# Keys of the next batch transposed earlier, in the PSUM bank of the AV products, with eight buffers instead of six

## Chip, cores and metric

The kernel runs on one core of one Trainium2 chip. The metric is the time of one execution on the device in microseconds; of several runs the median counts. The engines are named as the profile names them: PE (TensorE), DVE (VectorE), ACT (ScalarE), POOL (GpSimd), SP (SyncE, which here only issues DMA transfers). PEld is TensorE's loading of weights.

## What is computed

Attention with head mixing, then a routed mixture of experts, then a dense layer pair, on 4 batches of 448 tokens, 12 heads of 64. Only the first part bears on this change:

```python
scale = 1.0 / np.sqrt(q.shape[-1])
scores = scale * np.matmul(q, k.transpose(0, 1, 3, 2))
scores = np.einsum('bhij,hg->bgij', scores, w_pre)
scores = scores - np.max(scores, axis=-1, keepdims=True)
attn = np.exp(scores)
attn = attn / (np.sum(attn, axis=-1, keepdims=True) + 1e-09)
attn = np.einsum('bhij,hg->bgij', attn, w_post)
return np.matmul(attn, v).astype(np.float32)
```

The result, one row of 768 per token, goes to eight experts (`relu(x @ w1) @ w2`, the best expert of each token alone, weighted by its gate), and what comes out to `(h - tanh(h)) @ w_out` with `h = x @ w_in`.

## The kernel before

Each batch's 448 query rows are cut into tiles of 120, 120, 120 and 88 rows, 16 tiles T in all (T = 4b to 4b+3 are batch b's). A tile goes through these steps, named as in the code and, for their tiles, in the trace:

- `tr_q` (L297) turns the tile's queries for three pairs of heads at once into a PSUM bank (ptq); ACT copies them out as the high half qh (L304), DVE subtracts to get the low half ql (L305). `tr_k` (L281) does the same for the keys of one pair of heads and one whole batch: ptk, then kh on ACT (L287) and kl on DVE (L288). A pair is turned once per batch, six pairs in each.
- `emit_S` (L324) makes the scores of one pair of heads from three products (kh with qh, kl with qh, kh with ql). `emit_S2` makes two pairs: the first into the double bank "a", the second, one head each, into banks "d" and "e". ACT and DVE write them, scaled, to `ssb` in SBUF.
- A DMA on SP's queue (the relay, L354, seven rounds ahead) regroups ten query rows with all twelve heads on 120 partitions (`sr`). That is a block; the 16 tiles have 180, twelve or nine to a tile, 45 to a batch.
- For each block: P mixes the heads (L367, bank "b"); DVE takes the maximum (L369), ACT the exponential (L372); DVE makes the second mixing matrix with the row sums in it, w (L379 to L382); two rounds later T mixes and transposes (L404, bank "c") and ACT copies to A (L409).
- `emit_AV2` (L422) multiplies a whole tile's A by v for two pairs, into bank "d"; ACT copies that to xT (L424). `emit_X` (L456) turns xT and makes the router's products, half a tile at a time, in bank "e".
- `emit_R` routes the tokens of a batch, with small steps on DVE and PE. `conv_do` (L115 to L121) prepares weights of the dense part on DVE and POOL, about every second round.

Banks: PSUM has tags "a" (two banks), "b" and "c" (two each), "d" and "e" (one each). A tile in "d" or "e" can be written only when everybody has read the one before it there.

The order of instructions is written out. The loop over rounds s emits P of block s, then at most one score or AV step (`emit_S`, `emit_S2`, `emit_AV2`), then T of block s-2, then what else the round has: `tr_q`, `tr_k`, `emit_X`. Which round a step falls into is worked out ahead by `posS2`, `posAV` and the functions `at` and `at_e`; `at_e` moves a step to the next round that no other user of bank "e" has taken. The reading of such a late step's bank is put off to the next round: ACT's copy comes first in that round, DVE's part behind the reduce of the round's P and behind w. In these lines of the loop `flush()` gives out ACT's copies and `flush2()` DVE's subtractions:

```python
flush()
relay_to(s + NSR - 1)
ex = emit_P(s) if s < NBK else lambda: None
if 0 <= s - 1 < NBK:
    emit_W(s - 1)
flush2()
```

After the rounds come the experts, with their own pools in the memory that the attention stage gives back, and the dense layers.

Of the kernel before, what the change touches and what calls it, by code (L numbers as in the profile page):

```python
# [9 lines left out]
F32R = mybir.dt.float32r  # L10
# [20 lines left out]
def body(ctx: ExitStack, tc, q, k, v, w_pre, w_post, emb, tau, w1, w2, win, wout, out):  # L31
    nc = tc.nc
    pe, act, dve, pool, sp = nc.tensor, nc.scalar, nc.vector, nc.gpsimd, nc.sync
    B, H, S, D = q.shape
    NT = B * S
    DM = H * D
    E, _, FF = w1.shape
    F2 = wout.shape[0]
    CP, NJ = 112, 4
    NP = H // 2  # L40
# [13 lines left out]
    def ps(tag, nm):  # L54
        if len(PB) > 1:
            tag = {"a": "h", "b": "h"}.get(tag, "o")
        return psum[-1].tile([128, 512], F32, tag=tag, name=nm, bufs=PB[-1][tag])
# [67 lines left out]
    if True:  # L125
# [3 lines left out]
        ap = bctx.enter_context(tc.tile_pool(name="attnB", bufs=1, side="left"))  # L129
# [147 lines left out]
        def tr_k(b, p, tag="e"):  # L277
            src = nat.pop(("k", b, p))
            pt = ps(tag, f"ptk{b}_{p}")
            for c in range(NJ):  # L280
                pe.transpose(pt[:, c * CP:(c + 1) * CP], src[:, c].rearrange("p h d -> p (h d)"), ident[:CP, :CP])  # L281
            hi = ap.tile([128, S], F32R, tag="kh", name=f"kh{b}_{p}", bufs=6)
            lo = ap.tile([128, S], F32R, tag="kl", name=f"kl{b}_{p}", bufs=6)
            kT[b, p] = (hi, lo)

            def evac():
                act.copy(hi, pt[:, :S])  # L287
                return lambda: dve.tensor_sub(lo, pt[:, :S], hi.bitcast(F32))  # L288
            return evac
# [45 lines left out]
        for T in range(4 * B):  # L335
            n = IT[T % 4][1]
# [74 lines left out]
        xT = {}  # L411

        def emit_AV(T, p, cpy=act.copy, m=1):
            b, it = divmod(T, 4)
            n = IT[it][1]
            if p == 0:
                xT[T] = cp.tile([128, KD, 120], F32, tag="xT", name=f"xT{T}", bufs=2)
            pt = ps("d", f"AV{T}_{p}")
            for x in range(m):
                for c in range(NJ):  # L420
                    for hh in range(2):
                        pe.matmul(pt[64 * hh:64 * hh + 64, x * 120:x * 120 + n], vt[b, p + x][:, hh, c, :],  # L422
                                  A[T][:, c, 2 * (p + x) + hh, :n], start=c == 0, stop=c == NJ - 1)
            return lambda: cpy(xT[T][:, p:p + m, :n], pt[:, :m * 120].rearrange("d (x i) -> d x i", x=m)[:, :, :n])  # L424

        def emit_S2(T, p):

# [8 lines left out]
        def emit_AV2(T, p):  # L436
            return emit_AV(T, p, act.copy, 2)
# [174 lines left out]
    with mctx:  # L612
# [240 lines left out]
        def at(pos, fn, *a):  # L853
            side.setdefault(int(pos), []).append((fn, a))
# [3 lines left out]
        def at_e(pos, fn, *a):  # L858
            pos = int(pos)
            while pos in eused:  # L860
                pos += 1
            eused.add(pos)
            at(pos, fn, *a)
            return pos

        def posS(T, p):
            f, nb = (first[T - 1], ntile[T - 1]) if T else (-12, 12)
            return f - (5 if T > 1 else 3) + (p + 0.5) * nb / 6

        def posS2(T, p):  # L870
            return posS(T, p - p % 2 + 0.5)

        def posAV(T, p):
            f, nb = first[T + 1], ntile[T + 1]
            return f + LAG + 1 + p * nb / 6

        def at_s(pos, *a):
            pos = int(pos)
            eused.add(pos)
            at(pos, *a)  # L880

        for T in range(1, 4 * B):
            if T == 1:
                at_s(posS(T, 3), emit_S, T, 3)
                at_s(posS(T, 4), emit_S2, T, 4)
            else:
                for p in range(0, NP, 2):
                    at_s(posS2(T, p), emit_S2, T, p)
        for T in range(2, 4 * B):
            at(posS2(T, 0) - 6, load_q, T)  # L890
            at_e(posS2(T, 0) - 2, tr_q, T, 0)
            at_e(posS2(T, 2) - 2, tr_q, T, 1)
        for b in range(1, B):
            for p in range(NP):
                e = posS2(4 * b - 1, p) + 1
                at(e - 5, load_k, b, p)
                at_e(e, tr_k, b, p)
        for p in range(NP):
            for b in range(B):
                at(posAV(4 * b - 1, p) + 2 if b else 1 + p, load_v, b, p)  # L900
        for T in range(4 * B - 1):
            for p in range(0, NP, 2):
                at(posAV(T, p), emit_AV2, T, p)
            e = posAV(T, NP - 2)
            if T == 4 * B - 2:
                continue
            at_e(e + 1, emit_X, T, 0)
            e = at_e(e + 2, emit_X, T, 1) - 2
            for gi, (_, t1) in enumerate(RG[:-1]):
                if t1 == T + 1:  # L910
                    for x, y in enumerate((0, 2, 2, 4, 4)):
                        at(e + 5 + y, emit_R, gi, x)
# [32 lines left out]
        def flush(tag=None):  # L945
            keep = []
            while late:
                x = late.pop(0)
                if tag in (None, x[0]):
                    y = x[1]()  # L950
                    if x[0] == "e" and callable(y):
                        late2.append((x[0], y))
                else:
                    keep.append(x)
            late.extend(keep)
            if tag:
                flush2(tag)
# [3 lines left out]
        def flush2(tag=None):  # L961
            for x in late2[:]:
                if tag in (None, x[0]):
                    late2.remove(x)
                    x[1]()

        def run_fill(fn, a):
            tag = "d" if fn is emit_AV2 else "e"
            if fn is emit_S2:
                flush("d")  # L970
                flush("e")
            elif fn is not emit_S:
                flush(tag)
            e = fn(*a)
            if fn in (emit_S, emit_S2):
                e()
                if a[1] + (fn is emit_S2) == NP - 1:
                    sdone.add(a[0])
            else:
                late.append((tag, e))  # L980
# [5 lines left out]
        for fn in [f() for f in (tr_k(0, 0, "e"), tr_q(0, 0, "d"), tr_q(0, 1, "c"))]:  # L986
            fn()
        for p in range(NP):
            if p + 4 < NP:
                load_k(0, p + 4)  # L990
            if p == 1:
                load_q(1)
            if p + 1 < NP:
                tr_k(0, p + 1, "de"[p % 2])()()
            run_fill(emit_S, (0, p, (None, "bb", "cc")[p % 3]))
            for _ in range(2):
                if p >= 1:
                    next(pen, None)
# [6 lines left out]
        for p in range(3):  # L1005
            run_fill(emit_S, (1, p, (None, "cc")[p % 2]))
            for _ in range(2):
                next(pen, None)
        for _ in pen:
            pass  # L1010
        for s in range(NBK + LAG + 6):
# [14 lines left out]
            i = s - LAG  # L1026
            on = 0 <= i < NBK
            fill.sort(key=lambda x: x[0] not in (emit_S, emit_S2, emit_AV2))
            if fill and fill[0][0] in (emit_S, emit_S2, emit_AV2):
                run_fill(*fill.pop(0))  # L1030
# [24 lines left out]
        for p in range(3):  # L1055
            emit_AV(TL, p, dve.tensor_copy)()
        emit_X(TL - 1, 1)()
        emit_AV(TL, 3, dve.tensor_copy)()
        emit_X(TL, 0, dve.tensor_copy)()
        for p in range(4, NP):  # L1060
# [15 lines left out]
        for n, e in enumerate(items):  # L1076
# [32 lines left out]
            for ci, col in enumerate(cols):  # L1109
                y = mq[0].tile([128, DM], F32, tag="y", name=f"y{nm}_{ci}", bufs=2)  # L1110
# [268 lines left out]
```

## Time and profile before

| | us |
|---|---|
| median of 3 runs | 1391.91 (1390.22 to 1392.75) |
| the profiled execution's own time | 1395.11 |
| its span, first to last instruction | 1393.4 |
| PE busy, share of the span | 1316.0 (94%) |
| DVE busy | 1019.3 (73%) |
| ACT busy | 741.6 (53%) |
| first P of the 180 blocks, last P | 22.7, 529.3 |

The attention stage is the stretch from about 20 to 547 us; the experts and the dense layers follow. A row of a timeline has the start in us from the span's beginning, the length in us of the merged instructions, the engine, the source line, the operation, output and inputs with their sizes, the count, and in brackets the idle time ahead of the first of them with the engine and line that ended it. A row of a group has busy time in us and the mean of one in ns, then the engine's idle time ahead of such instructions in us and what ended most of it. A row of a stretch has its length, then for each engine its busy time with the number of instructions, then the granted clock of PE (1.00 is full), the DMA engines' busy share and the rate.

### The profile page before, as it was taken

The numbers are of one execution on the slowest core, as the hardware profiler recorded it, in microseconds if no ns is written. First come the engines' busy times: TensorE is split into PE (matmuls) and PEld (weight loads), VectorE is DVE, ScalarE is ACT, GpSimd is POOL, SyncE is SP. The second block draws the span as 40 slices with busy tenths as digits, with TensorE's granted clock in tenths as the row PEclk, the third lists the DMA queues.
The fourth block names the chain that finished last, engine by engine and source line by source line (L and its number), as shares of the span: only waits on it lengthen the run. The fifth ranks groups of instructions, "written<-read, shape, count | busy, mean of one in ns | idle before, by whom it ended". The sixth has DMA issues, their size and how long they took to land. (4 is left out here: it accounts for less than half of the span.)

```text
span 1393.4 us, 24972 instructions
## 1 busy us (share of the span) xinstructions
PE 1316.0 (94%) x9104; PEld 1145.6 (82%) x9104; DVE 1019.3 (73%) x2189; ACT 741.6 (53%) x1518; POOL 502.2 (36%) x495
## 2 busy tenths in 40 slices
PE   8998998999899996999999999789999999999998
PEld 5766766677677775999999998689999889999998
DVE  5776786678667765677776774588888787788886
ACT  6666666666666663454555444464444435544442
POOL 0232332333233314332333331464445344454432
PEclk9999999999999998999999999799999999999999
DMA  6875575566557555777877873422112133212102
GB/s 154 259 245 157 179 207 155 163 188 197 144 166 202 173 152 183 236 235 234 278 248 258 261 233 116 125 68 69 46 46 86 46 99 112 68 47 68 46 24 80
DMA packets 149412, 210.90 MB, mean 151 GB/s; under 512 B 54022, under 2 KB 109494, under 8 KB 149286
## 3 DMA queue, kind: packets, MB, share of 16 engines
q1 hardware_dynamic: 145104, 194.19, 45.4%
q0 software_dynamic: 2640, 12.19, 2.9%
q10 hardware_dynamic: 1542, 2.89, 0.6%
q8 instruction: 73, 1.20, 0.4%
q14 instruction: 53, 0.43, 0.1%
HBM read 135.70 MB, written 35.00 MB: 123 GB/s over the span
## 5 line engine op out<-in xcount | busy, mean ns | idle before, releaser
L120 POOL TENSOR_TENSOR cm<-cm,ct 128x256 f32<-128x256 f32 x96 | 70.2, 731 | 426.5 <-DVE ct L117 394.3
L404 PEld LDWEIGHTS T<-w,p 120*112 120x112 f32 (+1 forms) x1440 | 165.8, 177 | 64.9 <-issue 48.7
L404 PE MATMUL T<-w,p 120*112 120x120 f32 (+1 forms) x1440 | 185.0, 272 | 5.0 <-DVE w L382 3.0
L369 DVE TENSOR_REDUCE mx<-P 120x1 f32<-120x448 f32 x180 | 111.7, 621 | 87.9 <-PE P L367 86.9
L1219 POOL TENSOR_TENSOR gl<-th,gh 128x448 fp32r<-128x448 f32 x64 | 74.9, 1170 | 260.9 <-ACT gh L1218 191.7
L367 PE MATMUL P<-sr,wpre 120*120 120x448 f32 x360 | 166.2, 544 | 1.4 <-ACT p L372 1.4
L372 ACT ACTIVATE p<-P,mx 120x448 f32<-120x448 f32 x180 | 114.0, 633 | 99.6 <-DVE mx L379 87.8
L1270 PE MATMUL o<-woh,gh 128*128 128x384 f32 x448 | 152.8, 341 | 4.9 <-DVE acc L1276 4.9
L1239 ACT ACTIVATE u<-h 128x448 f32<-128x448 f32 x64 | 35.0, 548 | 223.1 <-PE h L1235 223.1
L1272 PE MATMUL o<-woh,gl 128*128 128x384 f32 x448 | 151.1, 337 | 0.0
L1271 PE MATMUL o<-wol,gh 128*128 128x384 f32 x448 | 151.1, 337 | 0.0
L1235 PE MATMUL h<-yh,wil 128*128 128x448 f32 x384 | 143.8, 374 | 3.5 <-POOL wil L1208 3.5
L1233 PE MATMUL h<-yh,wih 128*128 128x448 f32 x384 | 144.0, 375 | 1.2 <-ACT wih L1207 0.6
L1234 PE MATMUL h<-yl,wih 128*128 128x448 f32 x384 | 144.1, 375 | 0.5 <-DVE yl L1182 0.5
L1276 DVE TENSOR_TENSOR acc<-acc,o 128x384 f32<-128x384 f32 x196 | 106.9, 548 | 50.9 <-PE o L1272 50.9
L409 ACT COPY A<-T 112x480 f32<-112x480 f32 x180 | 101.4, 563 | 21.0 <-PE T L404 20.5
L684 PE MATMUL hi<-xhi,w1hi 128*128 128x256 f32 x384 | 108.6, 283 | 0.0
L685 PE MATMUL hi<-xli,w1hi 128*128 128x256 f32 x384 | 108.4, 282 | 0.0
L686 PE MATMUL hi<-xhi,w1li 128*128 128x256 f32 x384 | 108.2, 282 | 0.0
L422 PEld LDWEIGHTS AV<-A,v 112*64 112x64 f32 x1536 | 75.4, 139 | 23.8 <-issue 10.8
L667 PE MATMUL ypi<-w2hi,hhi 128*128 128x384 f32 x272 | 93.1, 342 | 0.1
L668 PE MATMUL ypi<-w2li,hhi 128*128 128x384 f32 x272 | 91.8, 338 | 0.5 <-DVE w2li L637 0.3
(223 smaller groups left out, 3278.1 us busy)
## 6 DMA issues: line engine op xcount, KB each, us to landing
sr<-ssb SPq DMA_DIRECT2D x176, 210.0 KB
r<-in_moe_w SPq DMA_DIRECT2D x72, 384.0 KB
r<-in_moe_w SPq DMA_DIRECT2D x52, 512.0 KB
craw<-in_moe_w_in SPq DMA_DIRECT2D x48, 256.0 KB
craw<-in_moe_w_out SPq DMA_DIRECT2D x48, 256.0 KB
raw<-wi_d SPq DMA_DIRECT2D x15, 768.0 KB
wor<-wo_d SPq DMA_DIRECT2D x15, 768.0 KB
wi_d<-cm SPq DMA_DIRECT2D x48, 128.0 KB
```

What stands on the lines that cost most here:

```text
L367: pe.matmul(pt[:n, :S], wpre[:n, :n], t[:n, :], start=True, stop=True)
L369: dve.tensor_reduce(mx[:n, 0:1], pt[:n, :S], op=ALU.max, axis=AX.X, negate=True)
L372: return lambda: act.activation(p[:n, :], pt[:n, :S], AF.Exp, bias=mx[:n, 0:1], scale=1.0, accum_out=mx[:n, 1:2])
L404: pe.matmul(pt[:CP, c * n:(c + 1) * n] if m == 10 else pv[:, c], p[:n, c * CP:(c + 1) * CP], w[:n, :] if m == 10 else wv, start=True, stop ...
L684: pe.matmul(pt[:, :256], wh[:, sl], xh[:, c, :], start=c == 0, stop=False)
L685: pe.matmul(pt[:, :256], wh[:, sl], xl[:, c, :], start=False, stop=False)
L1233: pe.matmul(pt[:, :S], wi[0][:, c, sl], yh[:, c, :], start=c == 0, stop=False)
L1234: pe.matmul(pt[:, :S], wi[0][:, c, sl], yl[:, c, :], start=False, stop=False)
L1235: pe.matmul(pt[:, :S], wi[1][:, c, sl], yh[:, c, :], start=False, stop=c == KD - 1)
L1270: pe.matmul(pt[:, :384], gh[:, sl], wo[0][:, f, n0:n0 + 384], start=f == 0, stop=False)
L1271: pe.matmul(pt[:, :384], gh[:, sl], wo[1][:, f, n0:n0 + 384], start=False, stop=False)
L1272: pe.matmul(pt[:, :384], gl[:, sl], wo[0][:, f, n0:n0 + 384], start=False, stop=f == GF - 1)
```

## The change

The key buffers kh and kl get eight places each instead of six. Where the six key pairs of batch b were turned, each one round or more after the score step of tile 4b-1 that read the same pair for the last time, they are now turned two pairs sooner, the first two six rounds ahead of that. The bank is now "d" instead of "e": `at_d` looks for a round in which no S and no AV uses "d", and the AV steps are entered before. The loads of the keys are moved with them, five rounds ahead of where a pair's round was sought. A reading that was put off comes out the same way for bank "d" as for bank "e" (`callable(y)` without a tag).

```diff
-            hi = ap.tile([128, S], F32R, tag="kh", name=f"kh{b}_{p}", bufs=6)
-            lo = ap.tile([128, S], F32R, tag="kl", name=f"kl{b}_{p}", bufs=6)
+            hi = ap.tile([128, S], F32R, tag="kh", name=f"kh{b}_{p}", bufs=8)
+            lo = ap.tile([128, S], F32R, tag="kl", name=f"kl{b}_{p}", bufs=8)
...
+        dused = set()
+
         def at_s(pos, *a):
             pos = int(pos)
             eused.add(pos)
+            dused.add(pos)
             at(pos, *a)
+
+        def at_av(pos, *a):
+            dused.add(int(pos))
+            at(pos, *a)
+
+        def at_d(pos, *a):
+            pos = int(pos)
+            while pos in dused:
+                pos += 1
+            dused.add(pos)
+            at(pos, *a)
+            return pos
...
+        for T in range(4 * B - 1):
+            for p in range(0, NP, 2):
+                at_av(posAV(T, p), emit_AV2, T, p)
         for b in range(1, B):
             for p in range(NP):
-                e = posS2(4 * b - 1, p) + 1
+
+                e = int(posS2(4 * b - 1, p - 2 if p > 1 else 0)) + 1 - (6 if p < 2 else 0)
                 at(e - 5, load_k, b, p)
-                at_e(e, tr_k, b, p)
+                e = at_d(e, tr_k, b, p)
...
         for T in range(4 * B - 1):
-            for p in range(0, NP, 2):
-                at(posAV(T, p), emit_AV2, T, p)
...
-                    if x[0] == "e" and callable(y):
+                    if callable(y):
...
-            tag = "d" if fn is emit_AV2 else "e"
+            tag = "d" if fn in (emit_AV2, tr_k) else "e"
...
-            e = fn(*a)
+            e = fn(*a, tag) if fn is tr_k else fn(*a)
```

For the first change of batch the key pairs 0 to 5 stood at the ends of rounds 22, 24, 26, 27, 31 and 34; they now stand at the ends of 16, 18, 22, 24, 26 and 28. The score steps stand in rounds 17, 21, 25, 29, 32 and 35 and the AV steps in 15, 19, 23, 27, 31 and 35, before and after. The X steps of tile 0 move from rounds 28 and 36 to 24 and 26, those of tile 1 from 37 and 39 to 36 and 37. The second and third change of batch stand 45 and 90 rounds later with the same pattern.

On PE, rounds 26 to 28 of the kernel before (in a name the first number of ptk is the batch and the second the pair, that of AV and X the tile, that of P, T, w and p the block):

```order
L367 MATMUL P26_1198<-sr26_912,wpre_124 120x448
L404 MATMUL T24_1209<-w24_1156,p24_1118 112x120 x4
L281 MATMUL ptk1_2_1215<-ident_67,natk1_2_984 128x112 x4
L367 MATMUL P27_1227<-sr27_956,wpre_124 120x448
L422 MATMUL AV1_0_1238<-A1_764,v0_0_390 64x120 x8
L422 MATMUL AV1_0_1238<-A1_764,v0_1_404 64x120 x8
L404 MATMUL T25_1265<-w25_1205,p25_1153 112x120 x4
L281 MATMUL ptk1_3_1272<-ident_67,natk1_3_987 128x112 x4
L367 MATMUL P28_1283<-sr28_992,wpre_124 120x448
L404 MATMUL T26_1294<-w26_1234,p26_1202 112x120 x4
L456 MATMUL X0_0_1300<-ien_151,xT0_784 120x136 x3
```

The same rounds of PE in the changed kernel:

```order
L367 MATMUL P26_1222<-sr26_935,wpre_124 120x448
L404 MATMUL T24_1233<-w24_1180,p24_1142 112x120 x4
L281 MATMUL ptk1_4_1239<-ident_67,natk1_4_1008 128x112 x4
L459 MATMUL X0_1_1246<-ien_151,xT0_790 120x136 x3
L367 MATMUL P27_1260<-sr27_980,wpre_124 120x448
L422 MATMUL AV1_0_1271<-A1_770,v0_0_390 64x120 x8
L422 MATMUL AV1_0_1271<-A1_770,v0_1_404 64x120 x8
L404 MATMUL T25_1298<-w25_1229,p25_1177 112x120 x4
L367 MATMUL P28_1308<-sr28_1016,wpre_124 120x448
L404 MATMUL T26_1318<-w26_1267,p26_1226 112x120 x4
L281 MATMUL ptk1_5_1324<-ident_67,natk1_5_1011 128x112 x4
```

Before, the pair ptk1_2 ahead of AV1_0 lay in bank "e" and AV1_0 in "d"; now the pair ptk1_4 at that place lies in "d", as AV1_0 does, and X0_0 and X0_1 come sooner.

On DVE, round 27 of the kernel before, from the reduce of P on:

```order
L369 TENSOR_REDUCE mx27_1229<-P27_1227 120x1
L379 TENSOR_SCALAR mx26_1200<-mx26_1200 120x1
L380 RECIPROCAL mx26_1200<-mx26_1200 120x1
L382 TENSOR_SCALAR w26_1234<-wpost_125,mx26_1200 120x120
L288 TENSOR_TENSOR kl1_2_1221<-ptk1_2_1215,kh1_2_1220 128x448
```

And in the changed kernel:

```order
L369 TENSOR_REDUCE mx27_1262<-P27_1260 120x1
L379 TENSOR_SCALAR mx26_1224<-mx26_1224 120x1
L380 RECIPROCAL mx26_1224<-mx26_1224 120x1
L382 TENSOR_SCALAR w26_1267<-wpost_125,mx26_1224 120x120
L288 TENSOR_TENSOR kl1_4_1245<-ptk1_4_1239,kh1_4_1244 128x448
```

Here another pair stands at the same place; its low half is still read out behind the reduce and behind w.

## Rows read from the trace of the kernel before

**Rows 1.** Stretches: second batch's rounds; the attention stage's end, two pieces.
```profile
145.10:278.60 133.50, 125.96 (x1093) 92.77 (x1092) 95.82 (x295) 85.88 (x202) 45.42 (x63) 1.00 0.61 176
...
529.30:533.26 3.96, 1.80 (x16) 1.25 (x14) 3.89 (x7) 1.18 (x3) 2.60 (x2) 1.00 0.33 127
533.27:536.67 3.40, 3.40 (x35) 3.16 (x33) 2.86 (x9) 1.18 (x3) 2.08 (x1) 0.50 0.43 152
```

**Rows 2.** Groups of PE's matmuls in the stretch 22.7 to 529.3 us.
```profile
L422 PE MATMUL AV<-A,v 112*64 112x120 f32 (+1 forms) x1408 | 78.0, 264 | 0.0
L324 PE MATMUL S<-kh,qh 64*120 64x448 f32 (+1 forms) x174 | 39.7, 412 | 8.3 <-DVE kl L288 8.3
...
L456 PE MATMUL X<-ien,xT 128*120 128x136 f32 (+1 forms) x168 | 24.5, 281 | 7.3 <-DVE ql L305 3.9 <-DVE kl L288 3.3
...
L281 PE MATMUL ptk<-ident,natk 112*128 112x112 f32 x72 | 10.0, 261 | 6.2 <-PE T L404 4.5 <-issue 1.7
```

**Rows 3.** Timeline of PE: P of rounds 62, 63 and 64.
```profile
191.46 0.92 PE L367 MATMUL P<-sr,wpre 120*120 120x448 f32 x2
...
194.64 0.92 PE L367 MATMUL P<-sr,wpre 120*120 120x448 f32 x2
...
196.21 0.92 PE L367 MATMUL P<-sr,wpre 120*120 120x448 f32 x2
```

**Rows 4.** Timeline of PE: rounds 68 to 70, start of 71, round 73, start of 74.
```profile
208.13 0.92 PE L367 MATMUL P<-sr,wpre 120*120 120x448 f32 x2
208.98 1.86 PE L422 MATMUL AV<-A,v 112*64 112x120 f32 x32
...
211.91 0.94 PE L367 MATMUL P<-sr,wpre 120*120 120x448 f32 x2
...
214.53 0.57 PE L281 MATMUL ptk<-ident,natk 112*128 112x112 f32 x4 [0.86 <-PE T L404]
214.94 0.92 PE L367 MATMUL P<-sr,wpre 120*120 120x448 f32 x2
...
217.79 0.41 PE L324 MATMUL S<-kh,qh 64*88 64x448 f32 x1 [0.94 <-DVE kl L288]
...
219.45 0.92 PE L367 MATMUL P<-sr,wpre 120*120 120x448 f32 x2
...
225.35 0.92 PE L367 MATMUL P<-sr,wpre 120*120 120x448 f32 x2
...
228.19 0.93 PE L456 MATMUL X<-ien,xT 128*120 128x136 f32 x6 [1.10 <-DVE kl L288]
228.95 0.92 PE L367 MATMUL P<-sr,wpre 120*120 120x448 f32 x2
```

**Rows 5.** Timeline of DVE in rounds 68, 69 and 70.
```profile
209.09 0.62 DVE L369 TENSOR_REDUCE mx<-P 120x1 f32<-120x448 f32 x1 [0.34 <-PE P L367]
...
210.20 0.62 DVE L288 TENSOR_TENSOR kl<-ptk,kh 128x448 fp32r<-128x448 f32 x1
...
212.89 0.62 DVE L369 TENSOR_REDUCE mx<-P 120x1 f32<-120x448 f32 x1 [0.95 <-PE P L367]
...
217.02 0.62 DVE L288 TENSOR_TENSOR kl<-ptk,kh 128x448 fp32r<-128x448 f32 x1
```

**Rows 6.** Timeline, SP's queue: four key loads.
```profile
214.18 2.66 SPq L146 DMA_DIRECT2D natk<-in_k  x4
```

**Rows 7.** Timeline of PE: P of rounds 111 and 112, of 156 and 157.
```profile
335.22 0.92 PE L367 MATMUL P<-sr,wpre 120*120 120x448 f32 x2
...
340.08 0.92 PE L367 MATMUL P<-sr,wpre 120*120 120x448 f32 x2
...
468.94 0.92 PE L367 MATMUL P<-sr,wpre 120*120 120x448 f32 x2
...
472.27 0.92 PE L367 MATMUL P<-sr,wpre 120*120 120x448 f32 x2
```

**Rows 8.** Timeline of PE: an AV block in the stretch from 533.27.
```profile
533.55 3.36 PE L422 MATMUL AV<-A,v 112*64 112x120 f32 x32
```

More of the change, by code (lines that the diff above doesn't have):

```diff
@@ L423, in emit_AV, with evac @@
                                   A[T][:, c, 2 * (p + x) + hh, :n], start=c == 0, stop=c == NJ - 1)
-            return lambda: cpy(xT[T][:, p:p + m, :n], pt[:, :m * 120].rearrange("d (x i) -> d x i", x=m)[:, :, :n])
+            def evac():
+                cpy(xT[T][:, p:p + m, :n], pt[:, :m * 120].rearrange("d (x i) -> d x i", x=m)[:, :, :n])
+            return evac
         def emit_S2(T, p):
@@ L892, in body @@
             at_e(posS2(T, 2) - 2, tr_q, T, 1)
+        for T in range(4 * B - 1):
+            for p in range(0, NP, 2):
+                at_av(posAV(T, p), emit_AV2, T, p)
         for b in range(1, B):
             for p in range(NP):
-                e = posS2(4 * b - 1, p) + 1
+                e = int(posS2(4 * b - 1, p - 2 if p > 1 else 0)) + 1 - (6 if p < 2 else 0)
                 at(e - 5, load_k, b, p)
-                at_e(e, tr_k, b, p)
+                e = at_d(e, tr_k, b, p)
+                assert e < int(posS2(4 * b, p)) - 1, (b, p, e)
         for p in range(NP):
```

## The prediction

> **What bounds the kernel now.** I read the table of stretches first, then the groups of TensorE's instructions with the idle time ahead of each, then TensorE's own timeline through one change of batch, then VectorE's beside it. A round is named by its block, 0 to 179, and begins with the matmul P of that block; P+x below is x us after P's row begins. In the second batch's stretch TensorE is busy 125.96 of 133.50 us, at a granted clock of 1.00, while VectorE is busy 95.82 and ScalarE 85.88 [rows 1]. TensorE is the bound, and it takes its instructions in the order written, so what it stands idle for in this stage is lost. Of its idle time in the attention stage, 8.3 us stand ahead of S and 3.3 us ahead of X, both for kl, the low half of a key pair that VectorE subtracts out of bank e; 6.2 us stand ahead of ptk, the key transposes themselves, and none ahead of AV [rows 2]. A plain round takes 196.21 - 194.64 = 1.57 us, a round with a double score step 194.64 - 191.46 = 3.18 us [rows 3].
>
> These waits have one cause. Bank e holds one tile. A tile turned into it at the end of a round is read by ScalarE and VectorE in the next, and VectorE's part stands behind that round's reduce of P and the making of w: reduce at 209.09, kl from 210.20 to 210.82 where P began at 208.13, so kl ends at P+2.69; in the round of 214.94 it ends at 217.64, P+2.70 [rows 4, 5]. The reduce can't begin before P has ended, so kl can hardly end sooner in this order. Whoever wants bank e one round after a key pair resumes at about P+2.85 (217.79) [rows 4].
>
> **What the change removes.** In each of three changes of batch six steps meet bank e too early: three S, one X, two ptk. Their price is the lengthening of the round, not the idle time printed. For S: 219.45 - 214.94 = 4.51 against 3.18, that is 1.33 us (0.94 is printed, since the matmul that writes bank d runs alone ahead of its partner in bank e) [rows 3, 4]; nine times, 12.0. For X: the round takes 228.95 - 225.35 = 3.60, less 1.57 and less X's own 0.76, that is 1.27 [rows 3, 4]; three times, 3.8. For ptk: 214.94 - 211.91 = 3.03, less 1.57 and 0.41, that is 1.05 [rows 3, 4]; six times, with 0.8 more for one that the group lists under "issue" with 1.7 [rows 2], 7.1. Sum: 22.9 us are there to be won.
>
> **What it adds.** The order lists show where the six pairs of a batch now stand: for the first change at the ends of rounds 16, 18, 22, 24, 26 and 28, in bank d. The next user of bank d is the round after, each time: S, AV, AV, S, AV, S. The new placing avoids rounds that use bank d themselves and looks at no neighbour. So nine S wait as before, now with both halves of their second pair: they resume at the same P+2.85, 12.0 us in all. Nine AV wait that had no wait: AV begins at 208.98, P+0.85, and in that very round a kl ends at P+2.69 [rows 4, 5], so it would resume at P+2.85, 2.0 us late. It is the same DVE sequence (second order list above), the same round, another bank. Nine times, 18.0. The bounds of one: below, the 1.05 of a ptk behind a query tile; above, 2.0 + 0.8, by the one ptk wait that ran 0.8 over the others [rows 2, 4]. I take 2.0, since its row is from AV rounds. Behind a waiting AV stand the T matmuls and the next P on TensorE; T's inputs are two rounds old, so nobody else is late sooner than by that wait, and nothing overtakes it.
>
> X of the first half of tile 4b-4 moves up to the end of round 24, behind the query transposes of round 23 in bank e. Today a ptk stands there and starts at P+2.62 (214.53 against 211.91) [rows 4]. In the changed order the key pair goes first, into bank d, without wait and for 0.41; X then waits from P+1.98 to P+2.62: 0.64, three times, 1.9 us. The other moved X have a free bank ahead of them: nothing. The 18 x 4 transposes, their 18 copies and subtractions are the same in number and size: nothing.
>
> The key loads go to SyncE six rounds earlier, past loads of the relay. A group of four issues takes SyncE 2.66 us [rows 6]; relay loads are issued seven rounds ahead of their P, 11 us even if all seven were plain, and the natk buffers that the moved loads fill have been read by then. I cost it at nothing, at worst 2.66 once per group. The two more pairs of buffers are filled one pair ahead: no work.
>
> **What comes back.** A wait of TensorE lets VectorE catch up. Where VectorE runs behind, at the routing of the first two batches, rounds 66 and 111 are long: round 111 takes 340.08 - 335.22 = 4.86 against 472.27 - 468.94 = 3.33 for the same content without a lag [rows 7]. The new 2.0 us wait stands two rounds ahead of each and should cover most of it: 1.5 in one, and about half that in the other, 2.2 us returned. Bounds: 0 and 3.
>
> **The sum.** Added 12.0 + 18.0 + 1.9 = 31.9, removed 22.9, returned 2.2: 6.8 us longer. The profiled execution took 1395.11 with a span of 1393.4, so its like becomes 1401.9; it lies 3.2 above the median of the runs, so the median goes from 1391.91 to 1398.7, 0.49% slower. With 0 to 3 us returned that is 1397.9 to 1400.9; with a third of the nine AV at their lower or their upper bound besides, this case alone covers 1395.0 to 1403.3.
>
> **Rivals.** (a) Faster. Everything hangs on when the AV resumes. Were kl made ahead of the reduce, in the 0.95 us and more that VectorE idles before it [rows 5], neither AV nor S would wait: 1.9 left of 31.9, so 1.9 - 22.9 - 2.2 = -23.2, 1368.7. With S waiting as now the sign turns where an AV waits less than (22.9 + 2.2 - 12.0 - 1.9) / 9 = 1.24 us, that is where kl ends by P+1.95 and not P+2.69. Against it: the order list has kl behind reduce and w in the changed kernel too, and no row in an AV round shows an earlier end. For it: only that VectorE has the idle time. Chance 0.10.
>
> (b) Even. The waits are 9.0 us more, but VectorE's lead undoes more than two rounds' lag: the waits of X and S for ql, the query's low half, are part of the 7.3 us ahead of X [rows 2]. If they all went, 7.3 - 3.3 = 4.0 us ahead of X besides the 2.2, the balance would be 2.8, 1394.7; with each AV resuming 0.3 us sooner besides it is even, 1392.0. Against it: the X that wait for ql lie before the key stretch or in the last batch, where nothing is moved. Chance 0.14.
>
> (c) Slower still, by the clock. The granted clock was 1.00 in the second batch's stretch, still 1.00 up to 533.26 and 0.50 in the stretch from 533.27, right after 3.96 us in which TensorE was busy 1.80 [rows 1]. The changed kernel has more and longer idle spells close together, in rounds 23 to 29: 2.0, 0.64, 1.33, 2.0, 1.33 us. At the lower of the two levels, 1.2 GHz instead of 2.4, an AV block takes 3.36 instead of 1.86 us [rows 4, 8], 1.5 us more per such stretch; one stretch in each batch gives 6.8 + 4.5, 1403.2, and one at every AV wait 1412. Against it: today's six waits per batch, up to 1.7 us [rows 2], left the clock at 1.00. The Trainium skill, "TensorE: Matmul & The Clock Gate", section "A second HAM failure mode: psum-queue depth-cycling", tells of a kernel whose TensorE paused briefly between groups of matmuls as it cycled through PSUM banks, and whose clock swung between half and full rate for it; that would make case (c) the likely one. The rows of this kernel don't bear it out for pauses of this size, so the sum leaves it out. Chance 0.10.
>
> That the keys don't go where the words say is no case of its own: the order list has them in the rounds named.
>
> **How the numbers follow.** Forecast 0.66, (a) 0.10, (b) 0.14, (c) 0.10. The time is the forecast's, 1398.7. For 8 in 10 the range takes the forecast with its bounds, most of (b), and (c) at one stretch per batch: 1392 to 1404.5. A measurement of this kernel can tell about 0.2%, 2.8 us. Faster takes (a) and a little of (b): 0.11; same most of (b): 0.13; slower the forecast and (c): 0.76.
>
> **What would show it.** In the changed profile the idle time ahead of AV should be about 9 x 1.9 us, put down to DVE kl, where it is 0.0 now; that ahead of ptk should be gone; S by kl should stay at nine waits; X by ql should rise by three. Rounds 66 and 111 should fall to 3.3 to 3.5 us. The stretch of a change of batch should be 2 to 3 us longer, the expert and dense stages as long as they are. I am wrong if AV shows under 1.2 us per wait, if kl stands ahead of the reduce, or if the clock's record shows 0.50 inside the attention stage.

## The result

The changed kernel takes 1407.43 us (median of 4 runs, 1404.43 to 1409.43) beside 1392.33 (1390.22 to 1394.95) for the kernel before: a ratio of 1.0106, 95% interval 1.0080 to 1.0131. It is slower, as forecast, by 15.1 us where 6.8 were forecast, and lies above the range. The profiled execution took 1406.91, with a span of 1405.2.

The attention stage, from the first row of P to the last, took 22.68 to 529.3 before, 506.6 us. It now runs from 22.85 to 544.07, 521.2 us, which is 14.6 more. The rest of the span is 861.1 us, 864.1 before; nothing was changed there, and over the other runs of this case it lies between 860.9 and 864.6. Three stretches of the changed kernel, the rounds of the first three batches, answer to [rows 1]. The columns are the stretch and its length, then busy us and instructions of PE, PEld, DVE, ACT and POOL, then the granted clock of TensorE, the DMA share and GB/s:

```profile
22.80:151.50 128.70, 115.51 (x909) 83.43 (x908) 82.64 (x252) 80.36 (x186) 33.89 (x47) 0.99 0.70 209
151.50:287.80 136.30, 124.89 (x1093) 92.31 (x1092) 96.67 (x295) 85.22 (x202) 45.15 (x63) 1.00 0.59 172
287.80:427.10 139.30, 127.87 (x1093) 94.95 (x1092) 95.29 (x292) 85.06 (x201) 43.12 (x61) 0.98 0.60 168
```

The second batch's stretch is 136.3 us, 133.5 before, at an unchanged clock of 1.00; TensorE's idle time rose from 7.5 to 11.4. In the first and the third the clock is below 1.00, which it was not before. The groups of TensorE's matmuls in the attention stage answer to [rows 2]:

```profile
L422 PE MATMUL AV<-A,v 112*64 112x120 f32 (+1 forms) x1408 | 79.6, 267 | 18.3 <-DVE kl L288 16.4 <-issue 1.9
...
L324 PE MATMUL S<-kh,qh 64*120 64x448 f32 (+1 forms) x174 | 37.1, 417 | 11.8 <-DVE kl L288 9.3 <-DVE lk L493 2.5
...
L459 PE MATMUL X<-ien,xT 128*120 128x136 f32 (+1 forms) x168 | 24.5, 282 | 5.5 <-DVE ql L305 5.5
...
L281 PE MATMUL ptk<-ident,natk 112*128 112x112 f32 x72 | 9.9, 259 | 0.0
```

The wait moved as the prediction said: 6.2 us ahead of ptk became none, none ahead of AV became 18.3 in nine waits, nine S still wait, and X waits for ql alone, seven times instead of four. Three of the waits are printed with another cause (S in rounds 62 and 107 with lk, AV in 113 with issue); there too TensorE resumes 0.11 to 0.15 us behind the end of kl. The mechanism can be read in round 68, the one of [rows 4, 5]. TensorE, P of round 68 to P of round 71:

```profile
217.98 0.92 PE L367 MATMUL P<-sr,wpre 120*120 120x448 f32 x2
...
220.83 1.86 PE L422 MATMUL AV<-A,v 112*64 112x120 f32 x32 [1.92 <-DVE kl L288]
...
223.76 0.94 PE L367 MATMUL P<-sr,wpre 120*120 120x448 f32 x2
...
226.43 0.93 PE L459 MATMUL X<-ien,xT 128*120 128x136 f32 x6 [0.52 <-DVE ql L305]
227.19 0.92 PE L367 MATMUL P<-sr,wpre 120*120 120x448 f32 x2
...
230.03 0.44 PE L324 MATMUL S<-kh,qh 64*88 64x448 f32 x2 [1.14 <-DVE kl L288]
...
231.71 0.92 PE L367 MATMUL P<-sr,wpre 120*120 120x448 f32 x2
```

and VectorE beside it:

```profile
218.95 0.62 DVE L369 TENSOR_REDUCE mx<-P 120x1 f32<-120x448 f32 x1 [0.33 <-PE P L367]
...
220.06 0.62 DVE L288 TENSOR_TENSOR kl<-ptk,kh 128x448 fp32r<-128x448 f32 x1
```

kl ends at P+2.70 and AV begins at P+2.85, 2.0 us later than in [rows 4]. S resumes at P+2.84 in the round of 227.19. What comes back came back as well. Round 111 answers to [rows 7]; it is now 351.67 - 348.34 = 3.33, as round 156 was before, where it had been 4.86:

```profile
348.34 0.92 PE L367 MATMUL P<-sr,wpre 120*120 120x448 f32 x2
...
351.67 0.92 PE L367 MATMUL P<-sr,wpre 120*120 120x448 f32 x2
```

What the prediction did not have are rounds 17 and 19. They took 3.17 and 3.78 before:

```profile
59.09 0.92 PE L367 MATMUL P<-sr,wpre 120*120 120x448 f32 x2
...
62.62 0.60 PE L324 MATMUL S<-kh,qh 64*120 64x448 f32 x2 [1.80 <-DVE kl L288]
...
65.63 1.21 PE L367 MATMUL P<-sr,wpre 120*120 120x448 f32 x2
67.88 0.92 PE L367 MATMUL P<-sr,wpre 120*120 120x448 f32 x2
...
71.41 1.86 PE L422 MATMUL AV<-A,v 112*64 112x120 f32 x32 [2.61 <-DVE kl L288]
...
74.34 0.94 PE L367 MATMUL P<-sr,wpre 120*120 120x448 f32 x2
```

Round 17 is 65.63 - 59.09 = 6.54 and round 19 is 74.34 - 67.88 = 6.46. Two things are in these rows. S and AV resume at P+3.53, not P+2.85; and in round 17 the instructions behind the wait are slower themselves (S 0.60 where 0.46 is usual, P 1.21 where 0.92 is). The record of the clock, as stretches of the changed kernel, in pairs (the 3.4 us ahead of a fall, and those at the lower level), and last the 3.5 us ahead of the AV of round 19:

```profile
59.40:62.80 3.40, 1.60 (x10) 0.68 (x10) 2.93 (x8) 1.94 (x5) 2.15 (x3) 1.00 0.82 211
62.80:66.20 3.40, 3.40 (x15) 2.60 (x14) 0.62 (x1) 1.49 (x4) 0.00 (x0) 0.50 0.87 268
...
370.00:373.40 3.40, 1.31 (x9) 0.62 (x8) 2.66 (x9) 2.91 (x9) 2.18 (x3) 1.00 0.19 56
373.41:376.80 3.39, 3.39 (x33) 3.09 (x33) 0.00 (x0) 0.00 (x0) 0.00 (x0) 0.50 0.81 215
...
380.25:383.65 3.40, 1.59 (x13) 0.83 (x12) 2.66 (x7) 1.58 (x3) 2.14 (x3) 1.00 0.18 44
383.65:387.05 3.40, 3.40 (x14) 2.36 (x11) 0.62 (x1) 1.72 (x4) 0.00 (x0) 0.50 0.32 103
...
67.90:71.40 3.50, 0.90 (x4) 0.19 (x3) 3.22 (x9) 2.03 (x6) 1.96 (x3) 1.00 0.97 296
```

Three times the clock stood at 0.50, 1.2 GHz of 2.4, inside the attention stage, in rounds 17, 117 and 119, each time right behind a wait for kl. TensorE had been busy 1.31 to 1.60 of 3.40 us. Ahead of the AV of round 19, in the last row, it was busy still less, 0.90 of 3.50, and the clock stayed at 1.00.

### The profile page after: what moved, and what is told of

It is laid out like the page before. It is cut to its first block, busy times and chain, and to the rows that moved or that the text cites. A ratio compares the mean times of both kernels' runs of the same rounds, so it can differ in the third digit from the quotient of the medians.

```text
span 1405.2 us, 24955 instructions
## 1 busy us (share of the span) xinstructions
PE 1316.5 (94%) x9104; PEld 1145.9 (82%) x9104; DVE 1021.3 (73%) x2189; ACT 741.1 (53%) x1518; POOL 501.9 (36%) x495
## 5 line engine op out<-in xcount | busy, mean ns | idle before, releaser
L120 POOL TENSOR_TENSOR cm<-cm,ct 128x256 f32<-128x256 f32 x96 | 70.2, 731 | 441.6 <-DVE ct L117 392.9
L409 ACT COPY A<-T 112x480 f32<-112x480 f32 x180 | 101.5, 564 | 23.0 <-PE T L404 22.7
L422 PE MATMUL AV<-A,v 112*64 112x120 f32 (+1 forms) x1536 | 86.8, 267 | 18.3 <-DVE kl L288 16.4
```

## Experiments

The theory after these readings: bank "d" of the AV steps is the cause, because kl ends behind the reduce in the very round whose AV wants the bank (A in the expectations); the pauses also bring the clock down (C); and in some rounds kl is later than P+2.70, since VectorE has more to do there. The rivals: that the two more buffers or the earlier rounds and loads cost by themselves, and that the clock has no part in it. Each expectation says what it calls by a letter.

**The subtractions ahead of the reduce, in the changed kernel.** The same line of code as in the next experiment is added to it:

```diff
             flush()
+            flush2()
             relay_to(s + NSR - 1)
```

> The changed kernel with the put-off subtractions of VectorE (kl, ql) given out ahead of the round's reduce of P instead of behind the reduce and w. Theory A (each new wait lasts until kl, and kl is late only because it stands behind the reduce and w): kl ends near P+1.5 instead of P+2.7 to P+3.4, so an AV waits about 0.65 us instead of 1.7 to 2.6, S hardly at all, the waits of X for ql go too, and TensorE's clock stays at 1.00 in the attention stage: 1375 to 1383 us. Theory B (bank d is late for another reason, such as the copy on ScalarE, or the time is lost elsewhere): the AV waits stay over 1.5 us and the time over 1400.

Measured: 1382.04 us (1379.05 to 1384.29), ratio to the kernel before 0.9919 (0.9894 to 0.9944). The sign turns with the order on VectorE, as rival (a) had it, but not by as much. The groups of TensorE:

```profile
L422 PE MATMUL AV<-A,v 112*64 112x120 f32 (+1 forms) x1492 | 83.9, 266 | 12.6 <-DVE kl L288 12.0 <-ACT ssb L328 0.3
...
L324 PE MATMUL S<-kh,qh 64*120 64x448 f32 (+1 forms) x174 | 36.8, 418 | 2.9 <-DVE kl L288 2.9
```

AV still waits nine times, 1.33 us in the mean where 0.65 was expected: kl ends at P+1.74 to P+2.66 in eight of the nine rounds and at P+3.37 in round 109. In six of them (19, 23, 64, 68, 109, 113) kl begins 0.03 to 0.04 us behind the end of ACT's copy kh, which it needs and which ends at P+1.32 to P+2.72, behind ACT's copies of T and its exponential. In rounds 27, 72 and 117 kh ends at P+0.62, and VectorE first works on L464, a small reduce of X's product that waited for another copy of ACT (L463). Against the expectation the clock did not stay at 1.00 either: it fell once, in round 109.

**The same line in the kernel before.**

> The kernel before with the same one step: kl and ql ahead of the reduce of P. Theory A: all 18 waits of S, X and ptk at the changes of batch fall to nearly nothing, 22.9 us by the sum of the prediction, and some of the waits for ql with them: 1364 to 1372 us. If the reduce, which then comes about 0.45 us later in such rounds, holds up the exponentials, the gain is smaller: 1372 to 1385. Theory B: no more than 5 us gained.

Measured: 1372.78 us (1372.01 to 1373.02), ratio 0.9853 (0.9831 to 0.9875), at the lower edge of the second range. Little is seen of that range's condition: from the first P to the last TensorE idles 4.4 us ahead of T, 2.9 in the kernel before. The groups:

```profile
L422 PE MATMUL AV<-A,v 112*64 112x120 f32 (+1 forms) x1536 | 84.2, 262 | 0.0
...
L324 PE MATMUL S<-kh,qh 64*120 64x448 f32 (+1 forms) x174 | 39.4, 415 | 2.7 <-DVE kl L288 2.7
```

This pair tells more than either alone: with VectorE's order the same in both, the change costs 1382.04 - 1372.78 = 9.3 us, and the AV group shows where, 12.6 us against none.

**The changed kernel with its pauses filled.** It computes the same; dummy matmuls into T's bank, which T overwrites, keep TensorE busy while S or AV waits behind a key pair:

```diff
+            if on:
+                emit_T(i)
             if fill and fill[0][0] in (emit_S, emit_S2, emit_AV2):
+                if on and any(x[0] is tr_k for x in side.get(s - 1, [])):
+                    for _ in range(8 if fill[0][0] is emit_AV2 else 5):
+                        pe.matmul(tev[i][0][:, :128], ident, ident, start=True, stop=True)
                 run_fill(*fill.pop(0))
...
-                emit_T(i)
```

> The changed kernel with matmuls of no use (identity by identity, into the bank that T of the round overwrites) put ahead of each AV and each double score step that follows a key pair: eight ahead of an AV, five ahead of an S, about 1.7 and 1.05 us, to fill the waits without lengthening them. Theory C (part of the loss is the clock, which fell to 0.50 three times in the attention stage since TensorE stood idle): the clock stays at 1.00 there, the rounds 17, 18, 117, 119 and 120 lose the 4.9 us that they hold over rounds of the same content at full clock: 1401 to 1404 us. Theory D (the clock's record is not what costs): 1407 or more.

Measured: 1403.34 us, the median of five runs (1400.96 to 1405.70; a sixth took 4601.69 and counts neither here nor in the ratio), ratio 1.0071 (1.0049 to 1.0092), as expected. By the two ratios the kernel with more work on TensorE is 0.35% shorter than the changed one; each ratio is uncertain by about 0.2%, so the rounds have to tell it. Its stretches of the same three batches:

```profile
22.10:149.20 127.10, 122.61 (x987) 91.88 (x986) 83.11 (x252) 80.11 (x186) 33.74 (x47) 1.00 0.71 212
149.20:285.60 136.40, 133.66 (x1171) 101.79 (x1170) 96.62 (x295) 85.01 (x202) 45.15 (x63) 1.00 0.59 172
285.60:422.00 136.40, 133.55 (x1171) 101.89 (x1170) 95.30 (x292) 84.73 (x201) 43.11 (x61) 1.00 0.60 172
```

The clock is 1.00 in all three, and the second batch, where the changed kernel's clock had not fallen, is as long as there (136.4 against 136.3). This prices the falls. Rounds 17, 18, 117, 119 and 120 took 6.54, 2.25, 7.32, 6.22 and 2.48 us in the changed kernel, 24.81 in all, and 5.23, 1.96, 5.71, 5.20 and 1.88, 19.98, with the pauses filled: 4.8 us for three falls, 1.6 each. The wait for the bank itself is still there, hidden in the fill. The last experiment gives the same price without any fill, so the clock's part is shown.

**Another bank for the pairs ahead of an AV round.** Three of the six pairs of each change go to bank "e" again, in the same rounds:

```diff
                 e = at_d(e, tr_k, b, p)
+                if any(x[0] is emit_AV2 for x in side.get(e + 1, [])):
+                    kbank[b, p] = "e"
+                    eused.add(e)
...
-            tag = "d" if fn in (emit_AV2, tr_k) else "e"
+            tag = kbank.get(a, "d") if fn is tr_k else "d" if fn is emit_AV2 else "e"
```

> The changed kernel with the pairs that stand in the round ahead of an AV (rounds 18, 22 and 26 and the same in the other two changes of batch) put into bank e, the others in bank d as they are; the second X of a batch's first tile goes one round later for it. Times of the transposes otherwise, loads and buffers as in the changed kernel. Theory A (the nine AV waits are the bank's): the AV waits go, 1.7 to 2.6 us each, 18 to 19 us in all, and the clock's drop in round 117 with them; rounds 66 and 111 get back about 2.2 us of lateness: 1384 to 1390 us, less than before. Theory B (the loss comes from turning the keys earlier, from their loads or from the larger buffers): 1400 or more.

Measured: 1387.91 us (1386.21 to 1391.97), ratio 0.9967 (0.9948 to 0.9986), as expected. The groups:

```profile
L422 PE MATMUL AV<-A,v 112*64 112x120 f32 (+1 forms) x1410 | 78.5, 264 | 0.0
...
L324 PE MATMUL S<-kh,qh 64*120 64x448 f32 (+1 forms) x176 | 37.5, 416 | 12.3 <-DVE kl L288 9.3 <-DVE lk L493 2.5 <-ACT ssb L331 0.4
```

The bank of nine pairs is worth 1407.43 - 1387.91 = 19.5 us, against 18.3 us of printed wait; the rest of the change is then 0.3% to the good. The 19.5 us are not the waits alone: the profile has one fall of the clock, in round 17, where the changed kernel had three. Rounds 66 and 111 take 4.43 each, together as much as in the kernel before: what TensorE does not wait, VectorE does not catch up, as the prediction's term said.

**The two more buffers alone**, in the kernel before:

```diff
-            hi = ap.tile([128, S], F32R, tag="kh", name=f"kh{b}_{p}", bufs=6)
-            lo = ap.tile([128, S], F32R, tag="kl", name=f"kl{b}_{p}", bufs=6)
+            hi = ap.tile([128, S], F32R, tag="kh", name=f"kh{b}_{p}", bufs=8)
+            lo = ap.tile([128, S], F32R, tag="kl", name=f"kl{b}_{p}", bufs=8)
```

> The kernel before with eight places for kh and kl instead of six, and nothing else. Theory A (bank d is the loss): no difference, within 2 us of the kernel before. Theory B (the larger buffers move other tiles in memory and cost time): 1397 us or more.

Measured: 1392.18 us, ratio 1.0001 (0.9990 to 1.0012), with the waits of [rows 2]: S 8.3, ptk 6.1. Buffers that nobody uses cost nothing.

**The earlier rounds, placed by their neighbours.** With eight buffers the pairs can be put into rounds whose next round does not want the pair's bank. The rounds are written out:

```diff
-                e = int(posS2(4 * b - 1, p - 2 if p > 1 else 0)) + 1 - (6 if p < 2 else 0)
+                e = 45 * (b - 1) + (14, 18, 22, 26, 33, 36)[p]
+                kbank[b, p] = "eeeedd"[p]
                 at(e - 5, load_k, b, p)
-                e = at_d(e, tr_k, b, p)
+                if p < 4:
+                    eused.add(e)
+                at(e, tr_k, b, p)
...
-            tag = "d" if fn in (emit_AV2, tr_k) else "e"
+            tag = kbank[a] if fn is tr_k else "d" if fn is emit_AV2 else "e"
```

> The same placing of the pairs with the subtractions where they stood, behind the reduce and w. Loads and the eight buffers are those of the changed kernel, turning still earlier for the first pair. Theory A (it matters alone who stands behind a pair in its bank): the 22.9 us go, one X per batch waits 1.2 us for ql behind the query tile: 1372 to 1377 us. Theory B (an early pair costs in itself): 1385 or more.

Measured: 1372.94 us (1370.27 to 1373.44), ratio 0.9855 (0.9839 to 0.9871), as expected. VectorE's order is that of the changed kernel here, and no wait for kl is left to speak of:

```profile
L324 PE MATMUL S<-kh,qh 64*120 64x448 f32 (+1 forms) x174 | 36.1, 411 | 0.4 <-DVE kl L288 0.4
...
L459 PE MATMUL X<-ien,xT 128*120 128x136 f32 (+1 forms) x192 | 28.2, 283 | 7.2 <-DVE ql L305 7.2
```

So turning keys early, with their loads early, is no loss in itself; with no neighbour hit, the waits for kl go and 1.45% is gained. What is left are the X that wait for ql. With the line of the first experiment besides:

> Key pairs placed by hand so that nobody wants their bank in the round after: for the first change of batch rounds 14, 18, 22 and 26 in bank e (each followed by an AV round, whose late step comes after kl), 33 and 36 in bank d (no S or AV in the round after); and the put-off subtractions ahead of the reduce, as in the second experiment. Theory A: no wait for kl or ql is left at the changes of batch, 22.9 us and the waits of X for ql, against the kernel before: 1363 to 1369 us, a few us under the early subtraction alone. If the early subtraction has taken all there is: 1371 to 1373.

Measured: **1365.13 us** (1364.82 to 1367.17), ratio 0.9810 (0.9794 to 0.9825), as expected. This version beats both kernels:

```profile
L422 PE MATMUL AV<-A,v 112*64 112x120 f32 (+1 forms) x1536 | 84.2, 262 | 0.9 <-ACT ssb L328 0.7
...
L324 PE MATMUL S<-kh,qh 64*120 64x448 f32 (+1 forms) x174 | 37.8, 413 | 0.1
...
L459 PE MATMUL X<-ien,xT 128*120 128x136 f32 (+1 forms) x192 | 28.0, 282 | 0.0
```

**Why kl was later still in rounds 17, 19, 23, 62 and 119.** VectorE in round 17 of the changed kernel:

```profile
60.33 0.62 DVE L369 TENSOR_REDUCE mx<-P 120x1 f32<-120x448 f32 x1
...
61.24 0.70 DVE L382 TENSOR_SCALAR w<-wpost,mx 120x120 f32<-120x120 f32 x1
...
61.86 0.61 DVE L288 TENSOR_TENSOR kl<-ptk,kh 128x448 fp32r<-128x448 f32 x1
```

and POOL beside it:

```profile
61.25 0.61 POOL L118 TENSOR_TENSOR cm<-craw 128x256 f32<-128x256 f32 x1
```

The reduce begins at P+1.24 where it could at P+0.97, behind a step of a weight conversion of the round before; and w takes 0.70 us. Over the changed kernel's trace w takes 0.28 us in all 110 cases with no POOL instruction beside it, and 0.68 in the mean beside L118 and L120 together. So kl ends at P+3.38, and in rounds 19 and 119 likewise; in 23 and 62 only the reduce is late and kl ends at P+2.96. The test moves a conversion one round ahead where a key pair is turned in its round:

```diff
+            if any(x[0] is tr_k for x in side.get(st, [])):
+                st -= 1
```

> The changed kernel with each weight conversion that stood in a key pair's round moved one round ahead, so that VectorE's three steps of it don't stand ahead of the next round's reduce. Theory E (in rounds 17, 19, 23, 62 and 119 kl ends up to 0.7 us later than P+2.69 because the conversion of the round before pushes the reduce by 0.27 and its POOL step falls on w, 0.70 instead of 0.28 us): kl ends near P+2.7 in all of these, 2.6 us less; and as the waits of S in rounds 17 and 119 fall from 1.80 to 1.14 us, the clock no longer drops there, 3.3 us less: 1400 to 1403 us. If the clock drops as before: 1404 to 1406. If kl's lateness has another cause: 1407.

Measured: 1403.46 us (1400.78 to 1405.66), ratio 1.0078 (1.0063 to 1.0093), just above the first range. Round 17 in it:

```profile
59.75 0.62 DVE L369 TENSOR_REDUCE mx<-P 120x1 f32<-120x448 f32 x1 [0.53 <-PE P L367]
...
60.67 0.28 DVE L382 TENSOR_SCALAR w<-wpost,mx 120x120 f32<-120x120 f32 x1
...
60.87 0.62 DVE L288 TENSOR_TENSOR kl<-ptk,kh 128x448 fp32r<-128x448 f32 x1
```

P began at 58.79; w is at 0.28 again, kl ends at P+2.70, and the round takes 4.55. Rounds 62 and 119 go with it (4.56 and 4.52). In this execution the clock fell in round 117 alone; as the next experiment shows, the rounds of the falls differ from one execution to the next, so this one profile does not show that the shorter waits kept the clock up in 17 and 119. Round 19 only went from 6.46 to 6.20, with kl ending at P+3.12: the reduce is back at P+0.96, but POOL's L118, which waited for its load, falls on w all the same:

```profile
67.18 0.71 DVE L382 TENSOR_SCALAR w<-wpost,mx 120x120 f32<-120x120 f32 x1
```

Round 23 gained nothing (6.09 for 6.04): there VectorE still works off the moved conversion and the reduce of the round before, kh ends at P+2.35 and kl at P+3.01. So the conversion is shown to be the cause in rounds 17, 62 and 119, and in 19 what is left is again w beside L118; for 23 the test shows nothing.

**The changed kernel twice more, unchanged**, one execution each, to see whether the clock falls in the same rounds.

> The changed kernel once more, unchanged. Theory C1 (the clock drops where a wait is long enough, whatever the run): 0.50 again in the rounds 17, 117 and 119. Theory C2 (it depends besides on when in time the wait falls, which differs from run to run): as many waits, but another number of drops or other places, and a time that differs from 1406.9 by 1.5 to 1.7 us for each.

> The same for a third time. C1: the same three rounds. C2: again other places or another number; the waits for kl in microseconds agree with the first run to 0.1 us in every round that the clock leaves alone.

Measured: 1414.42 and 1408.62 us, and 1395.20 for the kernel before beside them. The waits of S and AV agree with those of the first profile to 0.1 us. The falls don't: seven in the first repeat, in rounds 17, 23, 64, 72, 109, 113 and 119; in the second, four rounds, 19 (for 6.8 us), 23, 117 and 119. One stretch of the first repeat:

```profile
63.50:66.90 3.40, 3.40 (x13) 2.54 (x12) 0.62 (x1) 1.73 (x4) 0.00 (x0) 0.50 0.99 256
```

This gives the price of a fall within one program, without any fill. In the second repeat the clock stayed at 1.00 in rounds 17 and 18:

```profile
57.98 0.92 PE L367 MATMUL P<-sr,wpre 120*120 120x448 f32 x2
...
63.21 0.92 PE L367 MATMUL P<-sr,wpre 120*120 120x448 f32 x2
...
65.17 0.92 PE L367 MATMUL P<-sr,wpre 120*120 120x448 f32 x2
```

They take 5.23 and 1.96 us, as with the pauses filled, against 6.54 and 2.25 in the first profile: 1.6 us for the fall. Round 117 takes 5.71 in the first repeat, which had no fall there, and 7.32 in the first profile, 1.6 again. The attention stage lasts 521.2, 528.1 and 524.2 us with three, seven and four of them, which is 1.7 us for each of the four more in the first repeat. Which pauses let the clock fall is not settled by the program; how many there are moves the time by several us between executions.

## Why the prediction was right in sign and short in size

**Right: the mechanism.** AV waits in the nine rounds named, up to P+2.85 where nothing else delays kl (220.83 behind 217.98). Nine S wait as before. The waits ahead of ptk are gone. X behind the query transposes costs 0.69 in round 24 (0.64 forecast). Rounds 66 and 111 went from 4.00 and 4.86 to 3.33 each, 2.2 us returned, the forecast to the tenth.

**Right: what was costed at nothing.** The buffers cost nothing by themselves, and nor do the earlier rounds with their earlier loads: placed by bank and neighbour, the kernel is 1.45% shorter than the one before. Rivals (a) and (b) fell: kl stays behind the reduce, and the X waits for ql grew instead of going. But (a)'s lever is real: with kl ahead of the reduce the same placing gives a ratio of 0.9919. Its price was wrong: 1368.7 was forecast and 1382.04 measured, because AV and S still wait for kl there, 12.0 and 2.9 us; in most of these rounds kl then hangs on ACT's kh, which the working left out.

**Short: two terms of the sum.** S was 12.0 and is 13.8: in rounds 17, 62 and 119 the lengthening is 2.05, 1.64 and 2.06 and not 1.33 (17 and 119 at full clock, from the filled kernel). AV was 18.0 and is 19.0: the nine rounds grew by 17.8 at full clock (2.7 and 2.2 in rounds 19 and 23, 1.77 to 1.98 in the other seven), with 1.2 more for the three pairs of 0.41 us that have left rounds 27, 72 and 117. X was 1.9 and is 2.1. The sum with these is 13.8 + 19.0 + 2.1 - 22.9 - 2.2 = 9.8 us instead of 6.8. The step that failed there was to take kl's end from rounds 68 and 70 alone. The trace of the kernel before already had it later in two of the eighteen rounds, P+2.96 in round 23 and P+3.37 in round 117, both AV rounds, where no one waited for it:

```profile
355.71 0.92 PE L367 MATMUL P<-sr,wpre 120*120 120x448 f32 x2
...
358.47 0.61 DVE L288 TENSOR_TENSOR kl<-ptk,kh 128x448 fp32r<-128x448 f32 x1
```

**Wrong: the clock left out of the sum.** The prediction's own sign of being wrong, 0.50 inside the attention stage, came true. 9.8 us is not 14.6. The rest, 4.8 us, is what the three falls cost by the filled kernel, and 9.8 + 4.8 = 14.6 is what the attention stage grew by in the profiled execution; with another number of falls it grows by another amount. Rival (c) had this mechanism and a price, 1.5 us a fall and 1403.2 to 1412, and the measured time lies between its two ends; it got a chance of 0.10, and the range took only its lower end. The step that failed is the sentence against it, that today's six waits of up to 1.7 us left the clock at 1.00. Most of those waits are shorter than the new ones, which take 1.80 us ahead of S in round 17 and 1.92 to 2.61 ahead of AV in the rows shown. But the length of a wait does not decide it alone: the longest of the kernel before, 1.72 us ahead of a ptk, brought no fall, while a wait of 1.74 ahead of the AV of round 64 brought one in the first repeat and none in the first profile. The row that spoke for (c), a fall behind 3.96 us in which TensorE was busy 1.80 [rows 1], was the nearer one: 1.60 of 3.40 and 1.59 of 3.40 are what stands ahead of two of the new falls. The Trainium skill, "TensorE: Matmul & The Clock Gate", section "A second HAM failure mode: psum-queue depth-cycling", tells of short pauses from cycling through PSUM banks that make the clock swing; the falls of the changed kernel (0.50 in three stretches), and their absence in the one profile with the pauses filled, agree with it.

## What to carry to other kernels

When a tile is moved into another PSUM bank, look at who uses that bank in the next round and how late the last reader of the new tile ends; a search for a round in which the bank is free finds only the collisions in its own round. A row from one round gives the size of a wait for the quiet rounds alone: look at the same step in the rounds where the reading engines have something else to do. Where a change gives the engine that sets the time new pauses, cost them twice, once as waits and once as possible falls of its clock, and let the range reach over both.

## What was not expected of the hardware

The granted clock fell to 0.50 in three, seven and four rounds in three executions of the same program with the same waits. In the first profile TensorE was busy 1.31 to 1.60 of 3.40 us ahead of a fall; busy 0.90 of 3.50, in round 19, did not bring one there, and in the second repeat there was one in that round, beginning while AV still waited. What decides it stays open.

w, a product of 120x120 with one number per row, took 0.28 us wherever no POOL instruction ran beside it. In the changed kernel's trace 45 rows of w overlap one of POOL's L118, and 43 of them last 0.53 to 0.71 us and end 0.075 to 0.079 us behind L118, whether they begin 0.16 us behind it or 0.02 ahead of it. The two others keep 0.28: one begins 0.10 us ahead of L118, one just before L118 ends. The Trainium skill, "SBUF — State Buffer", section "Who interferes with whom", says that VectorE's tensor_scalar can, in its modes that use two ports, take the ports that it shares with GpSimd, and that whichever of the two comes second then stands still for the whole of the other's instruction. The rows agree in that w does not end before L118 does; which of the two came second can't be read from starts 0.02 us apart. But beside L120 alone w keeps its 0.28 us (five rows), and why L118 and L120 differ was not tried.
